# Spreading the softmax reciprocals by DRAM instead of by transposes, and a table load that waits for its group of sines

## The chip, the cores and the metric

The kernel runs on one core of a Trainium2 chip. The metric is the device time in microseconds of one execution. A profile is one execution recorded by the hardware; its engines are called TensorE (PE, with its weight loads as PEld), VectorE (DVE), ScalarE (ACT), GpSimd (POOL) and SyncE (SP, which issues most of the DMAs).

## The reference

Attention with a threshold, and on its result a mixing layer. B = 8 batches, H = 8 heads, S = 576 positions, D = 64, so the mixing layer has 512 channels.

```python
scores = (1 / sqrt(D)) * (q @ k.T)                    # per batch and head, 576 x 576
thresh = max(scores, axis=-1) - tau
scores = where(scores >= thresh, scores, -1e9)
attn = exp(scores - max(scores))
attn = attn / (sum(attn, axis=-1) + 1e-9)
x = attn @ v                                          # heads side by side: batch x 576 x 512
theta = x @ w_theta
y = w_tok_r @ (x * cos(theta)) + w_tok_i @ (x * sin(theta))
u = x + y
out = u + maximum(u @ w_ch, 0)
```

All of it is float32.

## The kernel before, in words

**Attention.** Heads go in pairs, 32 pairs (`n`), four to a batch (`NP = 4`). A pair's 576 rows of scores are cut into five units (`i` 0 to 4): units 0 to 3 have 128 rows of each of the two heads (`j` 0 and 1), unit 4 has the last 64 rows of both heads in one tile. That makes nine half units per pair, 288 in all, and the main loop runs over them as steps `t`. For one half unit, `score` forms the scores on TensorE (L278) in the one PSUM tile for scores, and VectorE evicts them (L282) with their negated minimum. `softmax` takes the exponential on ScalarE (L299), and VectorE multiplies by the mask (L300), which also sums the row into a column of the small tile `rows`. `flip` and `flip_last` transpose the result on TensorE (L326, L341) and ScalarE evicts it. `values` multiplies by v (L361), which gives the output transposed: 64 channels of each of the two heads on the 128 partitions, positions along the free axis, in a tile `xT` per pair.

**Normalization.** The row sums lie with positions on partitions, but `xT` has positions along the free axis, so their reciprocals must be turned and repeated over 64 partitions for each head. `invert` adds 1e-9, takes the reciprocals of the nine columns (L366, L367), and lets ScalarE widen eight of them to 64 copies each in a tile `rb` of 128 x 512 (L370). `normalize` transposes `rb` in four pieces on TensorE (L377), transposes the ninth column, repeated 128 times (L381), and multiplies `xT` by both from PSUM on VectorE (L383, L386).

**Mixing.** When the fourth pair of a batch is through, `split_x` splits the batch's four `xT` into high and low parts, and a generator `moe(b)` yields the mixing layer in small pieces: the angles (L402, evicted by ScalarE at L440, reduced to one turn on VectorE at L445 and L446), cosine and sine in two groups of two channel blocks, the transposes of the products (`z_ps`, L487, split at L489 and L490), the token products (`y_ps`, L504, added at L507), and the channel product (L402 again, added at L552), after which SyncE stores the block (L557). `fill`, called twice per step, takes as many pieces as a running account of due work allows, so the mixing of one batch fills TensorE between the steps of the next batch's attention.

**Sines.** In `sines`, for two channel blocks, VectorE takes an absolute value (L455) for the cosine, ScalarE loads the sine table (L459), runs two activations per block (L463, L464), and loads the exponential table back (L468). The helper `after` ties the sine table's load to the last absolute value, and the activations to the load, but only in the planned order: no semaphore makes the load wait.

**Order.** TensorE's order is the program's order, written out by hand: step `t` forms the scores of the half unit three ahead (`AHEAD = 3`), fills, transposes the half unit `t`, fills again, and does what `todo` holds for `t`. The other engines' order, the DMA queues among them, is planned ahead of time by priorities and simulated times. Every queue runs strictly in its order, so an instruction that waits holds all behind it. Query and key tiles are loaded by SyncE (L213) a pair ahead, value tiles at unit 4 (L244, L247). The tiles `qraw`, `kraw`, `th`, `km` and `rb` share four buffers of 128 x 576 (`temp`).

Of the kernel before, what the change touches and what calls it, by code (L numbers as in the profile page):

```python
# [10 lines left out]
F32 = mybir.dt.float32  # L11
F32R = mybir.dt.float32r
U32 = mybir.dt.uint32
AF = mybir.ActivationFunctionType
ALU = mybir.AluOpType
# [24 lines left out]
def tile_attn_moe(  # L40
# [11 lines left out]
    nc = tc.nc  # L52
    B, NP, D, _, S = qT.shape
    P = 128
# [7 lines left out]
    pool = ctx.enter_context(tc.tile_pool(name="pool", bufs=1))  # L62
    dram = ctx.enter_context(tc.tile_pool(name="dram", bufs=1, space=DRAM))
    ps_s = ctx.enter_context(tc.tile_pool(name="ps_s", bufs=1, space=PSUM))
    ps_t = ctx.enter_context(tc.tile_pool(name="ps_t", bufs=6, space=PSUM))
# [9 lines left out]
    ident = const.tile([P, P], F32, name="ident")  # L75
# [35 lines left out]
    def temp(name, dt=F32):  # L111
        return pool.tile([P, S], dt, tag="t576", name=name, bufs=4)

    def after(ins, other):

        info = mybir.DependencyInfo(mybir.DependencyClass.NoSync, mybir.DependencyReason.DATA)
        tc.add_manual_dep(ins.ins, other.ins.name, info, reason="order")
        return ins

# [87 lines left out]
    xT = {}  # L207
# [84 lines left out]
    def softmax(u, j):  # L292

        nm = u.nm
        nc.vector.tensor_scalar(
            out=nm[:, 2 + j : 3 + j], in0=nm[:, j : j + 1], scalar1=span, scalar2=None, op0=ALU.add
        )
        e = u.s[:, j]
        nc.scalar.activation(out=e, in_=u.ps[j], func=AF.Exp, bias=nm[:, j : j + 1], scale=-1.0)  # L299
        nc.vector.scalar_tensor_tensor(  # L300
            out=e,
            in0=u.ps[j],
            scalar=nm[:, 2 + j : 3 + j],
            in1=e,
            op0=ALU.is_le,
            op1=ALU.mult,
            accum_out=u.pr.rows[:, 2 * u.i + j : 2 * u.i + j + 1],
        )

    def group(pr, g):  # L310
# [53 lines left out]
    def invert(pr):  # L364
        rows = pr.rows
        nc.vector.tensor_scalar(out=rows[:, :9], in0=rows[:, :9], scalar1=1e-9, scalar2=None, op0=ALU.add)  # L366
        nc.vector.reciprocal(out=rows[:, :9], in_=rows[:, :9])  # L367
        rb = temp("rb")[:, :512]
        pr.rb = rb
        nc.scalar.copy(  # L370
            out=rb.rearrange("p (a b) -> p a b", b=64), in_=rows[:, :8].unsqueeze(2).broadcast_to([P, 8, 64])
        )

    def normalize(pr):
        tp = ps_t.tile([P, 512], F32, tag="t", name="rb_ps")
        for i in range(4):
            nc.tensor.transpose(  # L377
                out=tp[:, i * P : (i + 1) * P], in_=pr.rb[:, i * P : (i + 1) * P], identity=ident
            )
        tl = ps_t.tile([P, 512], F32, tag="t", name="rl_ps")  # L380
        nc.tensor.transpose(out=tl[:, :P], in_=pr.rows[:, 8:9].broadcast_to([P, P]), identity=ident)  # L381
        x = xT[pr.n]
        nc.vector.tensor_tensor(out=x[:, :512], in0=x[:, :512], in1=tp, op=ALU.mult)  # L383
        for j in range(2):
            r = slice(64 * j, 64 * j + 64)
            nc.vector.tensor_tensor(out=x[r, 512:S], in0=x[r, 512:S], in1=tl[r, 64 * j : 64 * j + 64], op=ALU.mult)  # L386


    def product(wm, parts, todo, together):

# [34 lines left out]
    def moe(b):  # L425
# [23 lines left out]
        def sines(ms):  # L449

            todo = []
            for m in ms:
                th = zs.pop((m, "f"))
                z = pool.tile([P, 2 * S], F32, tag="z", name="z", bufs=3)
                ab = nc.vector.tensor_scalar(  # L455
                    out=z[:, :S].bitcast(U32), in0=th.bitcast(U32), scalar1=0x7FFFFFFF, scalar2=None, op0=ALU.bitwise_and
                )
                todo.append((m, th, z))
            ahead_of = after(nc.scalar.preload_act_table(AF.Sin), ab)  # L459
            with tc.high_priority(offset=SINES):  # L460
                for m, th, z in todo:
                    ins = [
                        nc.scalar.activation(out=z[:, :S], in_=z[:, :S], func=AF.Sin, scale=-TURN_IN, bias=half_pi),  # L463
                        nc.scalar.activation(out=z[:, S:], in_=th, func=AF.Sin, scale=TURN_IN),  # L464
                    ]
                    for x in ins:
                        after(x, ahead_of)
                exp = nc.scalar.preload_act_table(AF.Exp)  # L468
                for x in ins:
                    after(exp, x)  # L470
            for m, th, z in todo:
                x = xT[b * NP + m]
                for i in range(2):
                    zi = z[:, i * S : i * S + S]
                    lo_eng.tensor_tensor(out=zi, in0=zi, in1=x, op=ALU.mult)  # L475
                zs[m] = z

        def flip(m):
            z = zs.pop(m)
            out = []  # L480
            for c0, nb in ((0, 4), (4, 1), (5, 4)):
                zh = pool.tile([P, nb, P], F32R, tag=f"zh{nb}", name="zh", bufs=4 if nb == 4 else 2)
                zl = pool.tile([P, nb, P], F32R, tag=f"zl{nb}", name="zl", bufs=4 if nb == 4 else 2)
                tp = ps_t.tile([P, 512], F32, tag="t", name="z_ps")
                for i in range(nb):
                    c = (c0 + i) * P
                    nc.tensor.transpose(out=tp[:, i * P : (i + 1) * P], in_=z[:, c : c + P], identity=ident)  # L487
                tv = tp[:, : nb * P].rearrange("p (c q) -> p c q", q=P)
                nc.scalar.copy(out=zh, in_=tv)  # L489
                nc.vector.tensor_tensor(out=zl, in0=tv, in1=zh.bitcast(F32), op=ALU.subtract)  # L490
                out += [(zh[:, i], zl[:, i]) for i in range(nb)]
                yield 110 * nb
            zs[m, "T"] = out
# [24 lines left out]
        for what in ORDER.split():  # L518
# [3 lines left out]
            if what == "a":  # L522
                other = flip(ms[1]) if turns else iter(())
# [11 lines left out]
            else:  # L535
                other = flip(ms[1]) if turns else iter(())
# [10 lines left out]
        for m in range(NM):  # L547
            wm = get_wm(1, m)
            u = xT[b * NP + m]
# [40 lines left out]
    def begin(n, i, j):  # L590
        if j == 0:
            units[n, i] = new_unit(n, i)
        u = units[n, i]
        score(u, j)
        softmax(u, j)
        if i == 4:
            invert(u.pr)
# [5 lines left out]
    todo = {}  # L603
    with tc.manual_schedule(engines={nc.tensor.engine}):
        with tc.high_priority(offset=ATTENTION):
            for x in halfs[:AHEAD]:
                begin(*x)
        for t, (n, i, j) in enumerate(halfs):
            pr = pairs[n]
            with tc.high_priority(offset=ATTENTION):  # L610
                if t + AHEAD < len(halfs):
                    begin(*halfs[t + AHEAD])
            fill()
            with tc.high_priority(offset=ATTENTION):
                u = units[n, i]
                flip(u, j)
                if j == 1 or i == 4:
                    flip_last(u)
                    del units[n, i]
            if (i, j) == (1, 1):  # L620
                todo.setdefault(t + 1, []).append((values, (pr, 0)))
            if i == 4:
                todo.setdefault(t + 1, []).extend([(values, (pr, 1)), (normalize, (pr,))])
                if n % NP == NP - 1:
                    todo.setdefault(t + LAG - 1, []).append((split_x, (n // NP,)))
                    todo.setdefault(t + LAG, []).append((lambda b: mixtures.append(moe(b)), (n // NP,)))
            fill()
            with tc.high_priority(offset=ATTENTION):
                for fn, a in todo.pop(t, ()):
                    fn(*a)  # L630
            if n + 1 < B * NP:
                if (i, j) == (0, 0):
                    prepare_q(n + 1)
                if (i, j) == (1, 0):
                    for jj in range(2):
                        prepare_k(n + 1, jj)
                if i == 4:
                    load_v(n + 1)
        with tc.high_priority(offset=ATTENTION):
            for t in sorted(todo):  # L640
                for fn, a in todo[t]:
                    fn(*a)
        for g in mixtures:
            for _ in g:
                pass
# [46 lines left out]
```

## Time and profile before

| | |
|---|---|
| time, three runs | 1160.13, 1164.57, 1164.94 us; median 1164.57 |
| span of the profiled execution | 1161.3 us |
| TensorE busy | 1054.1 us, 91% |
| VectorE busy | 833.7 us, 72% |
| ScalarE busy | 764.4 us, 66% |
| GpSimd busy | 369.1 us, 32% |
| DMA | 105.26 MB, 91 GB/s on average |
| TensorE's granted clock | 0.987 over the span |

The span reaches from the first to the last instruction of the profiled execution; its time is known by that span alone. In the profile a group of instructions stands under the line that issued it, as `out<-in`, with shapes, count, busy time, mean nanoseconds of one, then the idle time of its engine just before them and what ended it. Matmuls are pipelined, so their durations overlap. A row of the view of waits has the waiting instruction, what released it, the total in us, the number of times and the longest. A row of a timeline has its start and length in us, and in brackets the engine's idle time before it. A row of stretches has the stretch, its width, the busy us of PE, PEld, DVE, ACT and POOL with their counts, the granted clock, the share of the DMA engines and GB/s.

### The profile page before, as it was taken

The numbers are of one execution on the slowest core, as the hardware profiler recorded it, in microseconds if no ns is written. First come the engines' busy times: TensorE is split into PE (matmuls) and PEld (weight loads), VectorE is DVE, ScalarE is ACT, GpSimd is POOL, SyncE is SP. The second block draws the span as 40 slices with busy tenths as digits, with TensorE's granted clock in tenths as the row PEclk, the third lists the DMA queues.
The fourth block names the chain that finished last, engine by engine and source line by source line (L and its number), as shares of the span: only waits on it lengthen the run. The fifth ranks groups of instructions, "written<-read, shape, count | busy, mean of one in ns | idle before, by whom it ended". The sixth has DMA issues, their size and how long they took to land.

```text
span 1161.3 us, 21157 instructions
## 1 busy us (share of the span) xinstructions
PE 1054.1 (91%) x7736; PEld 923.7 (80%) x7736; DVE 833.7 (72%) x2107; ACT 764.4 (66%) x1434; POOL 369.1 (32%) x295
## 2 busy tenths in 40 slices
PE   4987888889989999899999999899989998899998
PEld 3565686778878888798878888788878988788898
DVE  7998876986767677765877667675877667676462
ACT  6656868655696667964697657865688655965350
POOL 2203125231352233522344233422335312530110
PEclk9989999989999999999999999999999999999999
DMA  7722222343332152212432142312432133310411
GB/s 254 203 84 77 63 71 62 118 141 99 108 96 62 32 165 86 80 42 77 129 115 63 31 137 84 100 52 60 144 86 83 42 101 101 98 32 1 127 60 60
DMA packets 55176, 105.26 MB, mean 91 GB/s; under 512 B 11936, under 2 KB 20128, under 8 KB 55072
## 3 DMA queue, kind: packets, MB, share of 16 engines
q1 hardware_dynamic: 45856, 70.35, 20.3%
q0 software_dynamic: 9216, 33.56, 10.1%
q8 instruction: 61, 1.00, 0.4%
q14 instruction: 43, 0.35, 0.1%
HBM read 90.24 MB, written 13.63 MB: 89 GB/s over the span
## 4 chain that ended last, share of the span: by engine, by line
PE 54%; ACT 18%; DVE 17%; DMA 5%; issue 5%; SPq 1%; ACTq 0%; DVEq 0%
PE y_ps L504 13%; PE m_ps L402 11%; PE s_ps L278 10%; PE o_ps L361 9%; PE t_ps L326 6%; DVE s_sb L300 4%; DVE sc L282 4%; ACT s_sb L299 3%; DMA qraw<-in_qT_dram 3%; ACT z L463 2%; DMA out_dram<-xT 2%; ACT L459 2%; ACT a L331 2%; ACT L468 2%; DVE th L446 2%
## 5 line engine op out<-in xcount | busy, mean ns | idle before, releaser
L300 DVE SCALAR_TENSOR_TENSOR s_sb<-sc,nm,s_sb 128x576 f32<-128x576 f32 x288 | 274.2, 952 | 107.2 <-ACT s_sb L299 103.0
L278 PE MATMUL s_ps<-k,qq 128*128 128x288 f32 (+1 forms) x1344 | 243.7, 309 | 61.6 <-DVE sc L282 41.2
L299 ACT ACTIVATE s_sb<-sc,nm 128x576 f32<-128x576 f32 x288 | 223.7, 779 | 105.7 <-DVE sc L282 104.8
L282 DVE TENSOR_SCALAR_CACHE_REDUCE sc<-s_ps 128x576 f32<-128x576 f32 x288 | 216.7, 752 | 80.9 <-PE s_ps L278 78.1
L278 PEld LDWEIGHTS s_ps<-k,qq 128*128 128x128 f32 x1344 | 194.5, 193 | 94.3 <-DVE sc L282 52.4
L331 ACT COPY a<-t_ps 128x512 f32<-128x512 f32 x256 | 148.4, 580 | 51.8 <-PE t_ps L326 51.1
L326 PE MATMUL t_ps<-ident,s_sb 128*128 128x128 f32 x1152 | 176.6, 276 | 5.3 <-DVE zl L490 5.0
L361 PE MATMUL o_ps<-a,v 128*64 128x320 f32 (+1 forms) x1280 | 170.2, 412 | 3.5 <-DVE xT L507 3.5
L504 PE MATMUL y_ps<-wt_h,zh 128*128 128x288 f32 x576 | 166.4, 307 | 4.6 <-ACT zh L489 3.8
L504 PE MATMUL y_ps<-wt_l,zh 128*128 128x288 f32 x576 | 164.2, 303 | 0.0
L326 PEld LDWEIGHTS t_ps<-ident,s_sb 128*128 128x128 f32 x1152 | 142.0, 142 | 10.2 <-DVE zl L490 7.1
L228 POOL TENSOR_TENSOR qq<-qraw,qq 64x576 fp32r<-64x576 f32 x62 | 101.8, 1642 | 140.5 <-ACT qq L226 85.9
L361 PEld LDWEIGHTS o_ps<-a,v 128*64 128x64 f32 x1280 | 88.8, 137 | 64.0 <-issue 7.2
L109 POOL TENSOR_TENSOR k<-kraw,k 128x576 fp32r<-128x576 f32 x62 | 90.9, 1466 | 145.4 <-ACT k L100 144.5
L192 POOL DMA_DIRECT2D wm<-wm_dram x64 | 36.5, 570 | 265.7 <-PE m_ps L402 234.0
L504 PEld LDWEIGHTS y_ps<-wt_h,zh 128*128 128x128 f32 x576 | 109.2, 190 | 6.7 <-ACT zh L489 4.4
L504 PEld LDWEIGHTS y_ps<-wt_l,zh 128*128 128x128 f32 x576 | 109.4, 190 | 0.0
L504 PE MATMUL y_ps<-wt_h,zl 128*128 128x288 f32 x576 | 103.5, 305 | 0.0
L402 PE MATMUL m_ps<-xh,wm 128*128 128x288 f32 x512 | 91.1, 307 | 8.8 <-ACT th L440 8.4
L402 PE MATMUL m_ps<-uh,wm 128*128 128x288 f32 x512 | 85.0, 301 | 11.9 <-ACT uh L100 11.9
L475 POOL TENSOR_TENSOR z<-z,xT 128x576 f32<-128x576 f32 x56 | 79.5, 1442 | 32.7 <-ACT z L463 22.9
L109 POOL TENSOR_TENSOR ul<-xT,uh 128x576 fp32r<-128x576 f32 x24 | 34.7, 1446 | 169.4 <-DVE uh L104 121.4
(85 smaller groups left out, 1608.5 us busy)
## 6 DMA issues: line engine op xcount, KB each, us to landing
wm<-wm_dram POOLq DMA_DIRECT2D x64, 512.0 KB, 4.2
qraw<-in_qT_dram SPq DMA_DIRECT2D x128, 144.0 KB, 3.0
kraw<-in_kT_dram SPq DMA_DIRECT2D x128, 144.0 KB, 2.9
out_dram<-xT SPq DMA_DIRECT2D x32, 288.0 KB, 4.3
v<-in_vp_dram SPq DMA_DIRECT2D x32, 256.0 KB, 2.8
wraw<-in_w_tok_dram SPq DMA_DIRECT2D x9, 576.0 KB, 4.7
wraw<-in_w_theta_dram SPq DMA_DIRECT2D x4, 512.0 KB, 5.4
wm_dram<-whi SPq DMA_DIRECT2D x8, 256.0 KB, 2.3
```

The source lines that it names most:

```text
L109: eng_lo.tensor_tensor(out=lo, in0=src, in1=hi.bitcast(F32), op=ALU.subtract)
L228: eng.tensor_tensor(out=qq[64:128], in0=raw[64:128], in1=qq[64:128].bitcast(F32), op=ALU.subtract)
L278: nc.tensor.matmul(ps[:, h, d0:d1], st, kk, start=(x == 0), stop=(x == len(todo) - 1))
L282: nc.vector.tensor_scalar(out=sc.rearrange("p (a b) -> p a b", a=2), in0=ps[:, :, :HS], scalar1=-1.0, scalar2=None, op0=ALU.mult, op1=ALU.min,
L299: nc.scalar.activation(out=e, in_=u.ps[j], func=AF.Exp, bias=nm[:, j : j + 1], scale=-1.0)
L300: nc.vector.scalar_tensor_tensor(out=e, in0=u.ps[j], scalar=nm[:, 2 + j : 3 + j], in1=e, op0=ALU.is_le, op1=ALU.mult, accum_out=u.pr.rows[ ...
L326: nc.tensor.transpose(out=tp[:, c * P : (c + 1) * P], in_=u.sf[:, k0 + c * P : k0 + (c + 1) * P], identity=ident)
L331: nc.scalar.copy(out=t.a[:, :, j, q0 : q0 + P], in_=tp.rearrange("p (c q) -> p c q", c=4))
L361: nc.tensor.matmul(o[64 * j : 64 * j + 64, :w], st, mv, start=(c == 0), stop=(c == 4))
L402: nc.tensor.matmul(tiles[h][:, :HS], wm[:, a, c, :], parts[c][bb][:, hs], start=(count[h] == 0), stop=(count[h] == 11))
L475: lo_eng.tensor_tensor(out=zi, in0=zi, in1=x, op=ALU.mult)
L504: nc.tensor.matmul(ps[:, :HS], z, w, start=(n == 0), stop=(n == len(work) - 1))
```

## The change

For the first three pairs of each batch the widened copy and the five transposes go. `spread`, called at the end of the step of unit 4 when what `todo` holds is done, transposes the nine columns of reciprocals in one go (9 x 128), ScalarE copies them out of PSUM, SyncE writes them as a line of 1152 values to DRAM, and four DMAs read that line back into the 128 x 576 tile `rb`, each head's part repeated over 64 partitions: 512 values and the last 64 for each of the two heads. `normalize` for these pairs is one multiply of `xT` by `rb` on VectorE, three steps after unit 4 instead of one. The fourth pair of a batch keeps the old way. The columns of `rows` are sorted by head, so that the line has each head's values in a row.

The second part gives `after` a true wait, used for the sine table's load alone: it now waits by a semaphore for the last absolute value of its group.

```diff
-    def after(ins, other):
-        info = mybir.DependencyInfo(mybir.DependencyClass.NoSync, mybir.DependencyReason.DATA)
+    def after(ins, other, wait=False):
+        kind = mybir.DependencyClass.Sync if wait else mybir.DependencyClass.NoSync
+        info = mybir.DependencyInfo(kind, mybir.DependencyReason.DATA)
...
+        col = 4 * j + u.i if u.i < 4 else 8
...
-            accum_out=u.pr.rows[:, 2 * u.i + j : 2 * u.i + j + 1],
+            accum_out=u.pr.rows[:, col : col + 1],
...
-        rb = temp("rb")[:, :512]
-        pr.rb = rb
-        nc.scalar.copy(
-            out=rb.rearrange("p (a b) -> p a b", b=64), in_=rows[:, :8].unsqueeze(2).broadcast_to([P, 8, 64])
-        )
+        if pr.n % NP == NP - 1:
+            rb = temp("rb")[:, :512]
+            pr.rb = rb
+            nc.scalar.copy(
+                out=rb.rearrange("p (i j b) -> p j i b", j=2, b=64),
+                in_=rows[:, :8].rearrange("p (j i) -> p j i", j=2).unsqueeze(3).broadcast_to([P, 2, 4, 64]),
+            )
+
+    def spread(pr):
+        tp = ps_t.tile([P, 512], F32, tag="t", name="r_ps")
+        nc.tensor.transpose(out=tp[:9, :P], in_=pr.rows[:, :9], identity=ident)
+        turned = pool.tile([9, P], F32, tag="turned", name="turned", bufs=2)
+        nc.scalar.copy(out=turned, in_=tp[:9, :P])
+        line = dram.tile([9, P], F32, tag="line", name="line", bufs=2)
+        nc.sync.dma_start(line, turned)
+        pr.rb = temp("rb")
+        flat = line.rearrange("a q -> (a q)")
+        for j in range(2):
+            r = slice(64 * j, 64 * j + 64)
+            for c, src, n in ((0, 512 * j, 512), (512, 1024 + 64 * j, 64)):
+                nc.sync.dma_start(pr.rb[r, c : c + n], flat[src : src + n].unsqueeze(0).broadcast_to([64, n]))
 
     def normalize(pr):
+        x = xT[pr.n]
+        if pr.n % NP < NP - 1:
+            nc.vector.tensor_tensor(out=x, in0=x, in1=pr.rb, op=ALU.mult)
+            return
...
-            ahead_of = after(nc.scalar.preload_act_table(AF.Sin), ab)
+            ahead_of = after(nc.scalar.preload_act_table(AF.Sin), ab, wait=True)
...
-                todo.setdefault(t + 1, []).extend([(values, (pr, 1)), (normalize, (pr,))])
+                todo.setdefault(t + 1, []).extend([(values, (pr, 1))])
+                todo.setdefault(t + (3 if n % NP < NP - 1 else 1), []).append((normalize, (pr,)))
...
                 for fn, a in todo.pop(t, ()):
                     fn(*a)
+                if i == 4 and n % NP < NP - 1:
+                    spread(pr)
```

More of the change, by code (lines that the diff above doesn't have):

```diff
@@ L381, in normalize @@
         nc.tensor.transpose(out=tl[:, :P], in_=pr.rows[:, 8:9].broadcast_to([P, P]), identity=ident)
-        x = xT[pr.n]
         nc.vector.tensor_tensor(out=x[:, :512], in0=x[:, :512], in1=tp, op=ALU.mult)
```

## The prediction, made before the changed kernel was run

> **What bounds the kernel now.** I read the page first (busy shares, slices, chain), then the stretches of 100 us, then who waited for whom, and last the timelines around one normalization and one group of sines.
>
> ```profile
> span 1161.3 us, 21157 instructions
> PE 1054.1 (91%) x7736; PEld 923.7 (80%) x7736; DVE 833.7 (72%) x2107; ACT 764.4 (66%) x1434; POOL 369.1 (32%) x295
> PE   4987888889989999899999999899989998899998
> PE 54%; ACT 18%; DVE 17%; DMA 5%; issue 5%; SPq 1%; ACTq 0%; DVEq 0%
> ...
> 300.00:400.00 100.00, 95.44 (x732) 85.17 (x731) 71.74 (x190) 72.87 (x136) 36.72 (x27) 1.00 0.25 72
> 500.00:600.00 100.00, 94.82 (x730) 84.72 (x728) 71.31 (x189) 64.84 (x126) 31.62 (x26) 1.00 0.29 85
> ...
> PE s_ps L278 <- DVE sc L282: 15.6, 15, 3.0
> PE m_ps L402 <- ACT th L440: 8.4, 7, 1.2
> PE z_ps L487 <- DVE zl L490: 4.9, 7, 0.8
> PE o_ps L361 <- DVE xT L507: 3.5, 7, 0.5
> PE s_ps L278 <- POOL k L109: 2.9, 6, 0.5
> ```
>
> TensorE bounds it. In a steady 100 us it is busy for some 95 (first column after the width), at a granted clock of 1.00, while VectorE and ScalarE stand near 71 and 65 to 73. The last five rows are TensorE's waits between 170 and 1060 us: in all that time the largest is 15.6 us. So an instruction taken off TensorE shortens the time almost one for one, and an instruction taken off ScalarE or VectorE shortens it only through those few waits. The first four slices are different (TensorE under 9 tenths): there VectorE sets the pace.
>
> **The change part by part.** First the transposes. Three pairs in four, 24 of 32, lose the four transposes of the widened reciprocals and the one of the ninth column, and get one transpose of nine rows.
>
> ```profile
> 520.53 0.69 PE L278 MATMUL s_ps<-k,qq 128*128 128x288 f32 x4
> ...
> 526.01 0.66 PE L377 MATMUL rb_ps<-ident,rb 128*128 128x128 f32 x4
> 526.51 0.27 PE L381 MATMUL rl_ps<-ident,rows 128*128 128x128 f32 x1
> 526.54 0.77 PE L278 MATMUL s_ps<-k,qq 128*128 128x288 f32 x4
> ...
> 531.87 0.69 PE L278 MATMUL s_ps<-k,qq 128*128 128x288 f32 x4
> ```
>
> The durations (0.27 us for one) overlap, so they are the wrong price. The right one is the distance of starts: the first of the five starts at 526.01, the scores behind them at 526.54, so five transposes occupy 0.53 us, 0.106 each. A transpose of nine rows still moves the 128 columns of the identity, so I price it like one of these, 0.106. TensorE loses 24 x (0.53 - 0.106) = 10.2 us. Its bounds are 24 x 0.53 = 12.7 us if the new one were free, and 24 x (0.53 - 0.27) = 6.2 us if it cost its whole duration. The reciprocals are ready long before the new transpose (the old copy that needs them already runs three half units ahead), so I add no wait.
>
> Next, ScalarE and VectorE:
>
> ```profile
> L370 ACT COPY rb<-rows 128x512 f32<-128x512 f32 x32 | 19.6, 611 | 2.9 <-DVE rows L367 2.9
> L344 ACT COPY a<-t_ps 128x128 f32<-128x128 f32 x128 | 34.3, 268 | 0.0
> L383 DVE TENSOR_TENSOR xT<-xT,rb_ps 128x512 f32<-128x512 f32 x32 | 21.8, 681 | 28.8 <-ACT xT L362 24.5 <-PE rb_ps L377 3.1 <-PE rl_ps L381 1.2
> L386 DVE TENSOR_TENSOR xT<-xT,rl_ps 64x64 f32<-64x64 f32 x64 | 13.7, 215 | 0.4
> L446 DVE TENSOR_TENSOR th<-th,km 128x576 f32<-128x576 f32 x32 | 33.0, 1032 | 1.0
> L109 POOL TENSOR_TENSOR k<-kraw,k 128x576 fp32r<-128x576 f32 x62 | 90.9, 1466 | 145.4 <-ACT k L100 144.5
> ```
>
> ScalarE drops a 611 ns copy and gains one out of PSUM of nine rows by 128, priced at 268 ns by the 128x128 one: 24 x 0.343 = 8.2 us less work. VectorE drops 681 + 2 x 215 = 1111 ns and gains one multiply of 128x576 with both inputs in SBUF. The nearest row with that shape is L446, 1032 ns on average: 24 x 0.08 = 2 us less, so nothing. Both lie beside TensorE's work and I count them as 0 us on the path. The normalization also moves two half units later, behind nothing that hurries: its consumer is the split of the whole batch, at the fourth pair, whose own normalization keeps its old form. So the 24.5 us that VectorE stood waiting for ScalarE's eviction L362 go for 24 of 32 pairs, about 18 us of VectorE idle time. What is late next there is the DMA, below.
>
> A rule speaks against the new multiply. L383 has one operand in PSUM and runs in 681 ns; L446 has two in SBUF and averages 1032. The Trainium skill, page "SBUF — State Buffer", section "Who interferes with whom", says that a VectorE instruction with two SBUF inputs contends with a GpSimd instruction that reads SBUF, and whoever came second is blocked. That the two-input row has the larger mean agrees. By L446's mean my sum is 1152; if each of the 24 had to sit out a whole GpSimd instruction (1466 ns), about 1.4 us more on VectorE per pair, three pairs in the VectorE-bound start would make it some 1156, and the steady part would hide the rest.
>
> Now the sine table:
>
> ```profile
> L299 ACT ACT_TABLE_LOAD x7 | 9.0, 1283 | 0.1
> L463 ACT ACT_TABLE_LOAD x7 | 9.0, 1283 | 0.1
> ...
> 170.96 1.28 ACT L459 ACT_TABLE_LOAD   x1
> 174.86 1.28 ACT L468 ACT_TABLE_LOAD   x1
> ...
> 190.72 1.28 ACT L459 ACT_TABLE_LOAD   x1
> 194.60 1.28 ACT L299 ACT_TABLE_LOAD   x1
> 196.68 1.28 ACT L463 ACT_TABLE_LOAD   x1
> 198.78 1.28 ACT L468 ACT_TABLE_LOAD   x1
> ```
>
> A group of four sines should cost two loads, one before and one after, as at 170.96 and 174.86, 5.2 us from start to end. In seven of sixteen groups the load was put ahead while the last absolute value was still unfinished. An exponential went into the hole, the exponential table came back (194.60) and the sine table again (196.68): 9.3 us. With a true wait the load is planned for when all four sines can run, and nothing fits between. ScalarE loses 7 x 2 x 1.283 = 18 us of loads. How much of that reaches the end? TensorE's waits that come right after such groups are the last three of the five rows above, 4.9 + 3.5 + 2.9 = 11.3 us, and that is the most to be had. On the other side, the clean groups also cost TensorE something: the 8.4 us in 7 waits for L440 stand behind unbroken blocks of sines, 1.2 us each. Seven broken groups turned into clean ones thus save 11.3 - 7 x 1.2 = 2.9 us, which I take. The wait itself can hurt: the load no longer overlaps the end of the absolute value, and behind it on ScalarE stand evictions and exponentials. At worst every load of sixteen comes later by a VectorE instruction of half a microsecond, -8 us. Bounds -8 to +11, taken +3.
>
> Last, the five DMAs per pair, 120 in all, on SyncE's queue:
>
> ```profile
> SPq L557 <- DVE xT L552: 263.5, 31, 52.2
> SPq L244 <- PE o_ps L361: 63.8, 22, 6.6
> ...
> 525.59 0.33 SPq L244 DMA_DIRECT2D v<-in_vp_dram  x1
> 526.11 1.77 SPq L247 DMA_DIRECT2D v<-in_vp_dram  x2
> ...
> L213 SPq DMA_DIRECT2D kraw<-in_kT_dram x128: 465/544/1567, 2.4 to 1027.6; - x128
> DMA to landing us min/median/max: 2.5/2.9/5.9
> wm_dram<-whi SPq DMA_DIRECT2D x8, 256.0 KB, 2.3
> ...
> DVE xT L383 <- ACT xT L362: 24.5, 14, 2.5
> ACT qraw L225 <- DMA qraw<-in_qT_dram: 21.8, 15, 3.3
> ```
>
> One issue takes 544 ns (median of the key loads), so 120 take 65 us of a queue that waits most of the time anyway (263.5 us for one line alone). What counts is when the spread row lands. The new transpose stands ahead of the scores at 520.53, the new multiply in program order ahead of those at 531.87: 11.3 us. The chain inside: transpose 0.3 and copy 0.3, up to 0.8 for ScalarE's instruction in hand; the write of the line, 2.3 by the nearest write to DRAM; four issues, the last starting 3 x 0.55 = 1.6 later; landing 2.9. That makes 8.2 us, 3 us inside the room. With the slowest landing of these rows (5.9) for both transfers it is 14.8, 3.5 us outside it. The new row of buffers is no tighter: the old widened tile was held from the reciprocals to the transposes, the new one from the DMAs to the multiply, both for some ten microseconds. I take 0 us for the DMAs, with bounds from 0 to the price of the first rival.
>
> **Sum.** -10.2 - 2.9 + 0 = -13.1 us on the profiled execution, 1161.3 to 1148. That execution's span lies 3.3 us under the median of the three runs (1164.57) and within their spread (1160.13 to 1164.94), so I take the 13 us off the median: 1152.
>
> **The rivals.** The first ends on the other side. VectorE's order is fixed ahead from planned times, and the multiply waits at its place in that order for a DMA. Everything behind it, the score evictions L282 that free the only score tile of TensorE, waits too. For: ScalarE was already caught like this, 15 of 64 query tiles were not there when their scale stood at the head (21.8 us, up to 3.3), and here two DMAs follow each other. SyncE's queue can add to it: the value loads L244 wait for TensorE until 525.59, and if they are put ahead of the spread's reads, those start at 527.9 and land at 527.9 + 1.6 + 2.9 = 532.4 instead of 528.7. Against: in the same place VectorE already waits for L362, up to 2.5 us, and TensorE's row for L282 is only 15.6 us. So about 2.5 us per pair are free. A wait of X costs 24 x (X - 2.5); it eats the 13 us at X = 3.0 and is slower by over 0.5% (5.8 us) from X = 3.3. At the queue's 3.7 us it is 24 x 1.2 = 29 us, or 1181. The Trainium skill, page "DMA: Bandwidth & Descriptors", section "Anatomy of one DMA — SWDGE (gpsimd) path", warns that completion "can cause a surprisingly long delay especially when the write target is HBM"; the write of 256 KB above, at 2.3 us, does not show it.
>
> The second: the time stays. TensorE's freed 10 us turn into its wait for the scores' eviction, because the ring from scores over eviction, exponential and mask back to TensorE is the next bound: row one of the waits grows from 15.6 to some 25 us, and the sines give nothing. For: the chain already holds 35% ScalarE and VectorE. Against: neither is above 73 of 100 us in the steady stretches. Some 1162.
>
> The third: the wait does not do what it says, an exponential still falls between the sines, because an input of theirs other than the absolute value is late. Against: both loads at 194.60 and 196.68 stand before the last sine only, the one that needs the last absolute value. Then 1164.6 - 10.2 = 1154.
>
> **How the numbers follow.** My forecast has 0.54 (1147 to 1158), the DMA rival 0.18, no change 0.20, the third 0.08. About 0.5% is what a measurement of this kernel can tell from no change, 5.8 us here: under 1158.8 is faster, over 1170.4 slower. Faster gets 0.54 + 0.08 = 0.62, the same 0.20, slower 0.18. The range starts at 1142, 10 us under the forecast (the bounds 12.7 and 11 of the two gains would give 1141), and reaches to 1174, into the DMA rival, so that about 0.12 of that rival and 0.05 below are left out.
>
> **What would show it.** Right: L377 and L381 fall to 8 pairs, TensorE's busy time falls by some ten microseconds, and its stretches stay near 95 of 100; table loads are 16 + 16 + 1, with none at L299 and L463; the waits for L490, L507 and the key's remainder shrink. Wrong: VectorE's new multiply shows a wait for the DMA over 3 us in most pairs, and TensorE's wait for L282 grows with it; or SyncE shows the spread's reads issued behind L244 or L557. A bare reshuffle of the planned order, with no row that fits any of these, would make the sum wrong by luck.

## The result, and the profile after

The changed kernel takes 1217.69 us (median; 1214.53 to 1220.5), the kernel before 1164.03 us beside it: a ratio of 1.0456, with a 95% interval from 1.0432 to 1.048. It is 54 us slower; the forecast was 12 us faster, and the range ended at 1174.

The page after, in the lines that answer to those of before (span, busy us, slices of TensorE and of its clock, chain):

```profile
span 1218.1 us, 21111 instructions
PE 1071.8 (88%) x7640; PEld 936.7 (77%) x7640; DVE 844.2 (69%) x2059; ACT 734.5 (60%) x1420; POOL 369.7 (30%) x295
PE   4877888898889988899998988899888989799998
PEclk9988998899999999899998999899998999999999
PE 42%; ACT 16%; DVE 16%; DMA 12%; issue 7%; SPq 5%; POOL 2%; ACTq 0%; DVEq 0%; POOLq 0%
```

TensorE has 96 matmuls less and yet 17.7 us more of busy time. DMA has grown from 5 to 12% of the chain, SyncE's queue from 1 to 5%. The same two stretches as before (columns as there):

```profile
300.00:400.00 100.00, 90.98 (x676) 80.66 (x673) 71.39 (x179) 65.37 (x127) 35.91 (x28) 0.97 0.25 74
500.00:600.00 100.00, 91.10 (x676) 81.67 (x676) 70.91 (x174) 56.73 (x114) 31.32 (x24) 0.95 0.30 87
```

TensorE gets 676 matmuls done where it did 730, and the clock, 1.00 before in both, is 0.97 and 0.95. The waits between 170 and 1060 us, the window of before's waits:

```profile
DVE xT L396 <- DMA rb<-line: 53.8, 17, 5.2
ACT qraw L226 <- DMA qraw<-in_qT_dram: 50.9, 25, 4.3
...
PE s_ps L279 <- DVE sc L283: 24.0, 21, 2.9
...
PE s_ps L279 <- POOL k L109: 18.5, 6, 3.3
...
PE m_ps L423 <- ACT uh L100: 16.0, 6, 3.0
...
PE z_ps L508 <- ACT th L461: 13.5, 7, 2.0
```

VectorE's new multiply (L396) waits for the spread row. ScalarE waits for query tiles more than twice as long as before (60.1 us in 31 waits over the whole span, where before's row in the prediction has 21.8 in 15). TensorE's own waits grow with them: for the scores' eviction, for the keys' remainder from GpSimd (2.9 us before), and ahead of the transposes behind the sines (L508; 4.9 us before, at L487). SyncE's queue, over the whole span, after and then before:

```profile
SPq L385 <- ACT turned L383: 409.4, 20, 28.7
SPq L578 <- DVE xT L573: 217.1, 32, 53.5
...
SPq L214 <- DVE th L467: 49.3, 7, 8.5
```

```profile
SPq L557 <- DVE xT L552: 263.5, 31, 52.2
SPq L213 <- DVE th L446: 217.8, 14, 29.7
SPq L213 <- POOL k L109: 152.1, 22, 15.2
SPq L213 <- POOL qq L228: 128.0, 22, 9.9
```

The queue now spends 409 us with the line's write (L385) at its head, which waits for ScalarE's copy `turned`. Before, it was the loads of queries and keys (L213) that stood there, 498 us in the last three rows, each waiting for the last user of the buffer that it was to fill: they were ahead of their use. One pair of the kernel after, first SyncE's issues, then one place where everything meets (in brackets the engine's idle time before the instruction and what ended it):

```profile
513.21 0.29 SPq L385 DMA_DIRECT2D line<-turned  x1
514.45 2.37 SPq L391 DMA_DIRECT2D rb<-line  x4
516.91 2.46 SPq L214 DMA_DIRECT2D qraw<-in_qT_dram  x4
519.47 2.46 SPq L214 DMA_DIRECT2D kraw<-in_kT_dram  x4
```

```profile
654.51 0.29 SPq L385 DMA_DIRECT2D line<-turned  x1
...
657.06 2.37 SPq L391 DMA_DIRECT2D rb<-line  x4
...
659.53 2.46 SPq L214 DMA_DIRECT2D qraw<-in_qT_dram  x4
...
661.84 0.76 DVE L396 TENSOR_TENSOR xT<-xT,rb 128x576 f32<-128x576 f32 x1 [5.22 <-DMA rb<-line]
...
663.26 0.77 ACT L226 ACTIVATE qraw<-qraw,small 128x576 f32<-128x576 f32 x1 [4.30 <-DMA qraw<-in_qT_dram]
...
663.32 1.17 PE L279 MATMUL s_ps<-k,qq 128*128 128x288 f32 x4 [1.95 <-DVE sc L283]
```

The query loads stand right behind the line and its four reads, and SyncE had issued nothing for 19 us ahead of 513.21. At 661.84 VectorE has waited 5.2 us for the row, at 663.26 ScalarE 4.3 us for its query tile, and TensorE stands 1.95 us for an eviction that was queued behind that multiply. The clock around this place (stretches; the clock stands after the five busy times):

```profile
652.00:660.12 8.12, 8.12 (x62) 6.42 (x61) 4.34 (x13) 3.65 (x9) 0.00 (x0) 1.00 0.12 27
660.12:663.53 3.41, 1.46 (x12) 1.23 (x11) 1.65 (x4) 0.27 (x1) 0.00 (x0) 1.00 0.68 196
663.53:666.94 3.41, 3.41 (x16) 3.39 (x16) 1.75 (x3) 3.41 (x7) 1.42 (x1) 0.50 0.79 238
```

TensorE was idle 1.95 of 3.41 us, and for the next 3.41 us it got half its clock.

The account of the span, taking as idle the time between TensorE's first and last instruction in which it neither multiplies nor loads weights: idle 93.7 us before, 132.9 after, +39; the rest of the span 1067.6 before, 1085.2 after, +18. If the transposes took away the 10 us of the prediction, the slower clock cost about 28, which is an estimate. Half-clock spells between these two instructions made 30.7 us in 7 before, none of them between 240 and 967 us, and 105.8 us in 23 after.

### The profile page after: what moved, and what is told of

It reads as the page before. It is cut to its first block, busy times and chain, and to the rows that moved or that the text cites. A ratio compares the mean times of both kernels' runs of the same rounds, so it can differ in the third digit from the quotient of the medians.

```text
span 1218.1 us, 21111 instructions
## 1 busy us (share of the span) xinstructions
PE 1071.8 (88%) x7640; PEld 936.7 (77%) x7640; DVE 844.2 (69%) x2059; ACT 734.5 (60%) x1420; POOL 369.7 (30%) x295
## 4 chain that ended last, share of the span: by engine, by line
PE 42%; ACT 16%; DVE 16%; DMA 12%; issue 7%; SPq 5%; POOL 2%; ACTq 0%; DVEq 0%; POOLq 0%
PE m_ps L423 11%; PE y_ps L525 9%; PE s_ps L279 9%; PE o_ps L363 6%; DMA qraw<-in_qT_dram 5%; PE t_ps L328 5%; DVE s_sb L302 4%; DVE sc L283 4%; SPq L391 4%; ACT s_sb L301 3%; DMA line<-turned 2%; POOL z L496 2%; DMA out_dram<-xT 2%; ACT qraw L226 2%; ACT a L333 1%
## 5 line engine op out<-in xcount | busy, mean ns | idle before, releaser
L302 DVE SCALAR_TENSOR_TENSOR s_sb<-sc,nm,s_sb 128x576 f32<-128x576 f32 x288 | 283.7, 986 | 110.9 <-ACT s_sb L301 106.5
L279 PE MATMUL s_ps<-k,qq 128*128 128x288 f32 (+1 forms) x1344 | 251.4, 315 | 95.7 <-DVE sc L283 54.1
L279 PEld LDWEIGHTS s_ps<-k,qq 128*128 128x128 f32 x1344 | 198.6, 197 | 141.6 <-DVE sc L283 64.0
L229 POOL TENSOR_TENSOR qq<-qraw,qq 64x576 fp32r<-64x576 f32 x62 | 96.9, 1563 | 297.4 <-ACT qq L227 241.6
L328 PE MATMUL t_ps<-ident,s_sb 128*128 128x128 f32 x1152 | 181.0, 282 | 0.8 <-ACT a L333 0.8
L363 PE MATMUL o_ps<-a,v 128*64 128x320 f32 (+1 forms) x1280 | 178.4, 427 | 0.9 <-DVE zl L511 0.8
L328 PEld LDWEIGHTS t_ps<-ident,s_sb 128*128 128x128 f32 x1152 | 147.2, 145 | 3.6 <-issue 1.5
L525 PE MATMUL y_ps<-wt_h,zl 128*128 128x288 f32 x576 | 110.0, 319 | 0.0
L364 ACT COPY xT<-o_ps 128x256 f32<-128x256 f32 x64 | 25.5, 398 | 109.2 <-PE o_ps L363 87.7
L525 PEld LDWEIGHTS y_ps<-wt_h,zl 128*128 128x128 f32 x576 | 89.9, 203 | 0.0
```

The source lines that it names most:

```text
L229: eng.tensor_tensor(out=qq[64:128], in0=raw[64:128], in1=qq[64:128].bitcast(F32), op=ALU.subtract)
L279: nc.tensor.matmul(ps[:, h, d0:d1], st, kk, start=(x == 0), stop=(x == len(todo) - 1))
L302: nc.vector.scalar_tensor_tensor(out=e, in0=u.ps[j], scalar=nm[:, 2 + j : 3 + j], in1=e, op0=ALU.is_le, op1=ALU.mult, accum_out=u.pr.rows[ ...
L328: nc.tensor.transpose(out=tp[:, c * P : (c + 1) * P], in_=u.sf[:, k0 + c * P : k0 + (c + 1) * P], identity=ident)
L363: nc.tensor.matmul(o[64 * j : 64 * j + 64, :w], st, mv, start=(c == 0), stop=(c == 4))
L525: nc.tensor.matmul(ps[:, :HS], z, w, start=(n == 0), stop=(n == len(work) - 1))
```

## The experiments

Two theories came from this. V: VectorE stands at the multiply until the row lands. S: SyncE's queue holds query and key loads behind the line's write. A third, W, was that the true wait of the sines hurts. In all that follows, ratios are to the kernel before on the same chip, with the 95% interval, and "idle" is TensorE's as above.

**The two parts apart.** The wait alone, in the kernel before (`after(..., ab, wait=True)` at the table load):

> The kernel before with the true wait of the sine table's load alone. Three theories for the 54 us lost (1164 to 1218): V, VectorE's new multiply stands in its queue for the spread row's DMA (61 us of waits in the changed kernel); S, SyncE's queue holds the query and key loads behind the spread's line write, which waits for ScalarE (409 us of waits); W, the true wait itself, because the unbroken block of sines delays what ScalarE and GpSimd owe TensorE (seven waits of 1.9 us for the products on GpSimd). V and S expect 1155 to 1166 here, with no table load at the exponential's line. W expects 1172 to 1190.

1167.7 us, 1.0041 [1.0023, 1.0059], between the ranges of the theories. The loads fell from 47 to 33 as the prediction said, and the time rose by 4 us all the same. GpSimd in this run, and TensorE's wait behind it:

```profile
477.89 5.58 POOL L476 TENSOR_TENSOR z<-z,xT 128x576 f32<-128x576 f32 x4 [3.22 <-issue]
483.44 3.81 POOL L109 TENSOR_TENSOR k<-kraw,k 128x576 fp32r<-128x576 f32 x2
```

```profile
PE s_ps L279 <- POOL k L109: 14.4, 7, 2.2
```

The four sines now run as a block, so GpSimd gets its four products as a block, 5.58 us, and the keys' remainder that TensorE needs stands behind it: 14.4 us where it was 2.9. The spread alone (the kernel after without the wait):

> The changed kernel without the true wait: the spread alone. V and S expect 1212 to 1228, as the changed kernel or a little more for the seven reloads that come back. W expects 1185 to 1205. VectorE's wait for the row's DMA should stay near 60 us in all of them.

1204.6 us, 1.0348 [1.0313, 1.0384]: 41 of the 54 us. The time is just inside W's range and under that of V and S, while VectorE still waited 45.4 us for the row and ScalarE 59.6 for queries. Only four groups of sines are broken here (41 table loads). The wait adds 13 us beside the spread, three times what it costs alone, so it is a part of the loss but the smaller one.

**S and V, cured one at a time.** The tile `rb` shares four buffers with the query and key tiles. Given its own, it can no longer tie the loads to itself:

```diff
-        pr.rb = temp("rb")
+        pr.rb = pool.tile([P, S], F32, tag="rbs", name="rb", bufs=1)
```

> The changed kernel with the spread row in a buffer of its own instead of one of the four shared with the query and key tiles. That puts the query and key loads ahead of the line write again in SyncE's queue; the multiply keeps its early place in VectorE's queue. S expects most of the loss back: 1170 to 1185, TensorE's waits for the key's remainder (20.8 us) back to some 3. V expects 1205 to 1218, with the 61 us of waits for the row's DMA unchanged.

1197.96 us, 1.0299 [1.0262, 1.0335], between the two theories. The waits over the whole span, the last row SyncE's own:

```profile
PE s_ps L279 <- DVE sc L283: 78.2, 56, 5.3
...
DVE xT L396 <- DMA rb<-line: 59.1, 17, 6.2
...
ACT qraw L226 <- DMA qraw<-in_qT_dram: 15.6, 13, 1.8
...
SPq L385 <- ACT turned L383: 98.9, 12, 26.2
```

The query tiles are there again (15.6 us), and the line's write stands at the head of SyncE's queue for 98.9 us in place of 409.4: S was right on what it said. VectorE's wait for the row is nearly as long as over the whole span of the kernel after (61.2 us in 20), and TensorE waits longer for the eviction behind it (there 54.1 us in 48). The multiply did not keep its early place, as the expectation had it: VectorE reached it 9.4 us (median) after the transpose, against 4.1 in the kernel after, but the line was written later too, 3.4 us against 1.3.

The other cure leaves the buffers shared and ties the multiply, in VectorE's order, behind the mask of the last half unit begun:

```diff
-            nc.vector.tensor_tensor(out=x, in0=x, in1=pr.rb, op=ALU.mult)
+            mul = nc.vector.tensor_tensor(out=x, in0=x, in1=pr.rb, op=ALU.mult)
+            after(mul, masks[-1])
```

> The changed kernel with the multiply tied, in VectorE's order, behind the mask of the half unit that was begun last, some 10 us after the transpose in place of some 4. SyncE's order keeps the query and key loads behind the line write. V expects the waits for the row's DMA to fall from 61 us to under 10 and the time to 1175 to 1190. S expects 1205 to 1220.

1244.32 us, 1.0693 [1.0627, 1.0758], the slowest of all and above both ranges. VectorE's wait for the row is gone, and that alone refutes V as the only cause. The row now holds its shared buffer longer, the loads come later (ScalarE waits 66.5 us in 32 waits), idle time is 152.8 us and half-clock time 129.7. Both cures together:

> Both cures together: the spread row in a buffer of its own, and the multiply tied behind the mask begun last; the sine table's true wait stays. If the two waits are the whole loss (the queue's 20 us as the own buffer gave back, VectorE's wait for the row the rest), VectorE waits under 10 us for the row, ScalarE under 25 us for the query tiles, and the time is 1152 to 1168: the 10 us of transposes less, the 4 us of the wait more. If the DMAs or the new order cost something by themselves, 1175 or more.

1164.85 us, 1.0021 [0.9999, 1.0044]; the loss is gone. VectorE never waits for the row, and the queries' row stands at:

```profile
ACT qraw L226 <- DMA qraw<-in_qT_dram: 14.6, 11, 1.8
```

The late multiply makes the time 27 us longer with shared buffers and 33 us shorter with its own: the two causes have to be cured together. The same without the true wait:

> The same without the true wait of the table's load. If the wait costs in this kernel what it cost alone (4 us) or beside the spread (13 us), this is the fastest of all, 1146 to 1160, under the kernel before. If the wait is neutral here, as the run above within 3 us.

1173.3 us, 1.0099 [1.008, 1.0119], with 47 table loads, outside both ranges. Here the wait gains 8 us, where alone it cost 4. Its sign depends on the order around it.

**What the chain costs by itself.** The old normalization everywhere, with the wait and the whole spread beside it, read into a buffer of its own that nobody uses:

> The old normalization for all pairs, one step after unit 4 as before, with the true wait, and beside it the whole chain of the spread (transpose, copy, line, four reads into a buffer of its own) whose result nobody reads. It prices the chain by itself: 24 transposes are 2.5 us, 24 copies lie on ScalarE, 120 issues on SyncE. Against the true wait alone (1168) the theory of two waits expects 1167 to 1176. If the DMAs themselves, or their place in SyncE's queue, cost the 20 us, 1185 or more.

1179.27 us, 1.0177 [1.0147, 1.0207], between the two expectations: by the ratios 1.4% or 16 us over the wait alone. ScalarE waits 29.5 us for queries, against 23.0 with the wait alone, although no one waits for the row. Whether the 16 us are the price of SyncE's extra issues or of the re-planned order is not shown: the control below with the widened tile in its own buffer lost as much with no DMA added.

**Another queue.** The line's write and its reads on GpSimd's queue (`nc.gpsimd.dma_start`), with shared buffers, first as planned and then with the late multiply:

> The changed kernel with the line write and the four reads on GpSimd's queue; the row stays in the four shared buffers and the multiply keeps its early place. If SyncE's order was what made the query and key loads late, ScalarE's waits for query tiles fall from 60 us to under 25 and the time to 1190 to 1205, as with the own buffer. If it was the shortage of shared buffers, they stay near 60 and the time at 1210 or more.

> The same with the late multiply. If the queue's order is what counts, 1160 to 1180, near the run with own buffer and late multiply. If the buffers are, 1230 or more, as the late multiply alone (1244), since the row then holds its shared buffer longest.

1185.01 us, 1.0166 [1.014, 1.0192], and 1196.04 us, 1.028 [1.0254, 1.0306]. The first lies below both of its ranges, the second between its two. Query waits fall to 34.7 and 30.6 us, halfway. GpSimd pays instead; its waits in the first of the two:

```profile
POOL rb L391 <- DMA line<-turned: 34.7, 16, 4.2
POOL line L385 <- ACT turned L383: 27.3, 16, 5.3
```

In the first VectorE waits only 5.8 us for the row, since the plan put the multiply later there (VectorE reached it 8.0 us after the transpose, by the median), so the second had little left to cure, and the first is no test of the queue alone. In the second TensorE's wait for the keys' remainder, GpSimd's work, is 19.3 us, against 9.7 in the first.

**Shortage or order?** The kernel after with five shared buffers in place of four (`bufs=5`):

> The changed kernel with five shared buffers in place of four, nothing else. If the loads are late because buffers are short, this helps as much as the buffer of its own (1198): 1190 to 1205, and ScalarE's waits for query tiles fall to some 20 us. If they are late because tiles of one shared set get their buffers in the program's order, so that a query tile can't be loaded before the spread row ahead of it has its buffer, SyncE's order stays (line, four reads, then the loads), the waits stay near 60 us and the time at 1208 to 1222.

1196.51 us, 1.0293 [1.0249, 1.0338]. The order on SyncE stayed (416.7 us at the head for `turned`, 53.9 us of query waits), as the order theory said; by the ratios (1.0456 and 1.0293) the time fell by about 19 us, as the shortage theory said. TensorE's wait for the keys' remainder fell from 20.9 to 8.0 us and VectorE's for the row from 61.2 to 52.3. How much of S is the one and how much the other stays open.

**Controls.** The kernel before, with its own widened tile `rb` moved to a buffer of its own:

> The kernel before with its widened tile of reciprocals in a buffer of its own, nothing else: a control, since a fifth buffer may help by itself. If the four shared buffers were short already, 1150 to 1158; if not, 1160 to 1166. What this gains has to be taken off the gain of the own buffer in the changed kernel.

1178.85 us, 1.0157 [1.0133, 1.0181]: slower by 17 us, which I had not expected. TensorE's program is the same; apart from the buffer only the planned order of the other engines changed (this run has 33 table loads without any true wait). So a private buffer is no gain by itself, and a re-planned order alone moves this kernel by more than the whole predicted gain.

In the version with both cures TensorE's largest wait besides the scores' eviction was for the products of the sines on GpSimd (L499): 13.2 us of idle time. The first channel block's products go to VectorE, with both cures and the wait, without the wait, in the kernel before, and in the kernel before with the wait:

```diff
-                    lo_eng.tensor_tensor(out=zi, in0=zi, in1=x, op=ALU.mult)
+                    (nc.vector if m == 0 else lo_eng).tensor_tensor(out=zi, in0=zi, in1=x, op=ALU.mult)
```

> Own buffer, late multiply and true wait, and the two products of the first channel block after the sines go to VectorE in place of GpSimd. In the kernel with both cures TensorE still waits 13.2 us in seven places for GpSimd's products, right after the block of sines. If those waits are a price of the block of sines and nothing else stands behind them, they vanish and the time is 1145 to 1156, faster than the kernel before. If another wait takes their place, 1158 to 1168.

> Own buffer, late multiply, no true wait, first block's products on VectorE. Without the move of the products this was 1173, with the true wait and the move 1165. If the move is worth the 6 us that it brought the kernel before, 1165 to 1169; if the broken groups of sines cost most here, 1155 to 1163.

> Control: the kernel before with the same move of the first block's products to VectorE, nothing else. It has no such wait, so 1158 to 1168; under 1155 would mean that the move is worth as much without the spread.

> The kernel before with the true wait and the move of the first block's products to VectorE. The wait alone cost 4 us because GpSimd does its four products in one block just ahead of the keys' remainders (14.4 us of TensorE's waits). If that is its price, the move takes half of the second group's block... only the first block of the first group is moved, so the keys' remainders behind the second group still wait: 1158 to 1166. Under 1155 the wait was harmful only through the first group.

With both cures and the wait: 1164.88 us, 1.0004 [0.9986, 1.0022]. The idle time stayed, 12.8 us of it now ended by the angles' eviction (L464), which stands on ScalarE behind the unbroken block of sines, so GpSimd alone was not the cause. The profile gave a hint of it: with both cures the weight loads waited for GpSimd, but the multiplications behind them already for L464 (13.4 us in 7). Without the wait: 1163.59 us, 0.9987 [0.9963, 1.0011], between its two ranges. The kernel before with this move: 1157.3 us, 0.9936 [0.9915, 0.9957], the only version whose whole interval lies under the kernel before; it has neither the spread nor the wait. With the wait added to it: 1163.02 us, 0.9993 [0.9973, 1.0013], and TensorE's wait for the keys' remainder is back at 14.0 us.

## Why the prediction was wrong, step by step

**TensorE bounds it: right.** That is also why every wait of another engine that reached it was paid in full.

**Transposes, -10.2: right in kind.** The 96 matmuls are gone. With both cures TensorE's time outside its idle gaps is 1061.6 us against 1067.6, although 47.8 us of it, not 30.7, ran at half clock. The gain was there, but even with both causes cured more idle time (101.3 us against 93.7) ate it. The true wait is not what added it: the same kernel without the wait has 104.2 us.

**The new multiply: no cost, as taken, and its price too high.** Taken at 1032 ns, it measured 772, in the groups of the kernel after:

```profile
L396 DVE TENSOR_TENSOR xT<-xT,rb 128x576 f32<-128x576 f32 x24 | 18.5, 772 | 67.9 <-DMA rb<-line 61.2 <-ACT xT L364 6.7
L480 ACT ACT_TABLE_LOAD x16 | 20.5, 1283 | 8.9 <-DVE z L476 8.6
L489 ACT ACT_TABLE_LOAD x16 | 20.5, 1283 | 0.3
```

The 1032 ns were a mean of two kinds: of the 32 instructions of L446, 24 took 750 to 759 ns and eight 1851 to 1859. During each of these eight a GpSimd instruction was running that had begun 0.2 to 0.4 us earlier. Where GpSimd's L228 began some 0.1 us after L446 instead, L446 took 757 to 759 and L228 some 1.95 us, against 1.4 in its shortest cases. So the blocking of whoever comes second, which the prediction weighed, is there in this kernel. The new multiply met it once (1107 ns, behind an instruction of L229); the other 23 took 742 to 760.

**Sine table, -2.9: the loads right, the term wrong.** 16 + 16 + 1 loads, as forecast; +4 us alone. Two of the three waits that I credited, for L490 and L507 (4.9 + 3.5 us), are gone in the run of the wait alone, and the one for the angles rose only from 8.4 to 9.6. The third, 2.9 us for the keys' remainder, became 14.4. I credited the waits that the broken groups caused and did not ask who is fed by an unbroken one: GpSimd's block of four products, ahead of the keys' remainder. The result lies within the bounds I gave (-8 to +11 of gain).

**"I take 0 us for the DMAs", "the new row of buffers is no tighter": the step that failed.** I compared how long a buffer is held, not what its first writer waits for. The old first writer was a ScalarE copy. The new one is a DMA on SyncE's queue that stands behind the line's write, so the next loads, which share the buffers, were put behind both; with the row in a buffer of its own they stood ahead of the line again. The queue that "waits most of the time anyway" was waiting with the loads at its head; now it waits 409 us with the line at its head and the loads behind.

**The chain, 8.2 us inside a room of 11.3: the length right for two pairs of three, the room not there.** From the second batch on it took, from transpose to multiply, 6.3 to 8 us for the later pairs of a batch, with two exceptions (10.3 and 9.1). For the first pair it took 11.6 to 12.6: the copy `turned` began 5.5 us after the transpose, behind the sines' block of 5.2 us on ScalarE, where the prediction allowed 0.8 for one instruction in hand. But program order does not hold VectorE: by the planned order it reached the multiply before the row was there in 20 of 24 pairs, and waited 3.06 us on average. Only the tie behind the mask made the room real.

**Rival one, 0.18, had V's mechanism and the wrong price.** It took 2.5 us per pair as free, by the longest wait that went. The total of that row, 24.5 us over 32 pairs, is 0.8. With that figure and the 59.1 us of the run with its own buffer (2.5 us for each of 24 pairs), the price would have been 24 x 1.7 = 41 us; the cure was worth 33. Its sign, over 3 us in most pairs, came in 9 of 24. "VectorE already waits" was true of 14 waits in 32 pairs, not of each. The SyncE order that the rival named, reads behind the value loads, was not the one that came: it was the loads behind the reads.

**Rival two, 0.20, fits the kernel with both cures.** It expected the time to stay and TensorE's wait for the scores' eviction to grow from 15.6 to some 25 us. With both cures, in the same window:

```profile
PE s_ps L279 <- DVE sc L283: 24.5, 27, 3.0
```

The time is 1164.85, and no version with the spread and both cures is clearly under the kernel before. That the ring through the eviction is the reason is not shown: the wait of 13.2 us for the products of the sines stands beside it, and the sines' part is unsettled, since the true wait gains 8 us in this version.

**The clock: not in the prediction.** I read 1.00 as given. It held between 240 and 960 us, where TensorE's gaps were 1.6 us at most.

Open: the split of S into shortage and order; how much of each ratio is the re-planned order, the 16 us of the unused chain among them; and whether the clock could be kept with the same idle time in other places, which no run tried.

## What to carry to other kernels

When data starts to go by DRAM, look first at which queue and which set of buffers its new first writer stands in: a write that waits for a late engine holds all later loads of an in-order queue, though the queue is idle. Then tie the consumer's place explicitly, since a later place in the program is no later place in a planned order, and price a wait that it replaces by its mean, not by its longest. A smaller count on the bounding engine is worth only what the planner's new order leaves of it; here a re-planned order alone cost 17 us.

## What the runs showed of the hardware

TensorE's clock needs less than a long pause to fall. All 23 half-clock spells of the kernel after last 3.41 or 6.83 us and start on one fixed grid of 3.41 us. Each follows a stretch of that grid in which TensorE was idle for 1.70 us or more in sum, and a single gap of 1.95 us was enough (the stretches at 660.12 above). Longer gaps that fell on the border of two stretches, 2.59 us at 273.5 and 2.53 at 556.5, left at most 1.6 us of idle time in either, and no spell followed; 3.00 us at 986.0, with some 1.7 in one of its two, gave none either. The kernel before had gaps of up to 1.6 us twice a batch (one of them its wait for L100, 11.9 us in 8) and no such spell between 240 and 967 us. The Trainium skill, page "TensorE: Matmul & The Clock Gate", section "HAM oscillation — how this bites in real kernels", gives the rule "no PE-idle gaps >~3.4µs"; by it the gap of 1.95 us would have cost nothing beyond itself, and the trace does not agree. The Trainium skill's section "A second HAM failure mode: psum-queue depth-cycling" on that page, where frequent small idle times make the clock swing, fits these spells better.

A small write to DRAM is fast: in 17 of 24 pairs the reads of the line were issued 1.2 to 1.4 us after the issue of its write (513.21 to 514.45), where the prediction took 2.3 for the write. Four issues on SyncE took mostly 2.4 to 2.5 us, 0.6 each.
